# The inverse transform's scratch turned round, and the whole issue order laid out anew

## The chip, the cores and the metric

The kernel runs on one core of a Trainium2 chip. Its time is the device time of one execution in microseconds; 618.68 us is the median of three runs of the kernel before (617.52 to 621.3). One execution was also recorded by the hardware profiler; the views quoted below come from that one.

## The reference, cut to what matters

The result mixes two branches row by row with a gate. One is a long convolution along the sequence (2048 rows, 512 channels) with a kernel K built from a state-space model with 128 states; the other is a gated linear unit with a hidden width of 1792.

```python
g = _sigmoid((x * gate_w).sum(-1, keepdims=True))
# a: the convolution
P = jnp.exp(logdA[:, :, None] * l[None, None, :])
K = jnp.einsum("dn,dnl,dn->dl", Cc, P, dB).real
...
Yf = Uf * Kf[None, :, :, :]
y = irfft2(Yf)[:, :, 0, :L]
a = y + u * Dskip
# b: the gated unit
h = _sigmoid(x @ w_gate) * (x @ w_up)
b = h @ w_down
return g * a + (1 - g) * b
```

## The kernel before, in words

Everything is done in one launch, and the two branches are interleaved instruction by instruction. The gated unit gives TensorE most of its work: `gups` (line 1125) multiplies x by the gate and up weights, `dps` (line 1197) multiplies the hidden tile by the down weights, each as three products of split operands. One turn of `gups` is six matmuls, one turn of `dps` three. Its weights are loaded by SyncE into staging tiles `st` (line 1055) and split into a high and a low part by ScalarE (line 1058) and VectorE (line 1059). The results of four groups of hidden slices are added into `out`: by a plain store, by accumulating DMAs issued from GpSimd (line 1221), and for the second half of the rows in the late groups by VectorE into tiles held in on-chip memory (line 1210; GpSimd and SyncE then don't add there, and SyncE stores the held tile at line 950).

The convolution is a transform of length 2048 made of small matmuls, with three scratch tensors in HBM between its steps:

- `rows` folds and transforms u (PE line 736) and stores the result in `a_u` (line 775).
- `tables` builds the kernel's terms by doubling (VectorE lines 608 to 610, ScalarE line 580) and multiplies them (PE line 652). `second` transforms them (PE line 682) and stores `a_k` (line 694).
- `passes` goes over two halves j of the channels (256 each) and four steps p2. Each step loads its part of `a_u` and `a_k`, finishes both transforms (PE lines 845 and 872), multiplies them (VectorE, from line 885) and does the first step of the inverse (PE line 910). `evict` copies that from PSUM into a tile `ev` (line 354) and stores it in the scratch `b_s` in two transfers of 256 KB (line 930), 32 of them in all.
- `finals` loads `b_s` when all 16 stores of its half j have landed: four blocks `t4`, each as four transfers of 256 KB (line 972), 32 in all. `last` does the last step of the inverse (PE `fps`, line 985), sums and differences on VectorE (lines 996 to 1003), and adds the gated result into `out`, by accumulating DMAs from GpSimd (line 1018) or into the held tiles (line 1008).

`b_s` is indexed by part c, q, j, then k (64 values) and channel. A store takes 64 partitions with four values of k each, which lie side by side: 4 KB without a break per partition. A load takes k on 64 partitions and four values of j, which lie 64 KB apart: four pieces of 1 KB per partition.

The tile `ev` has its own slots, and they are shared: the result tile `mn` of `last` comes out of the same pool of slots (line 991), and so a slot is free for the next `ev` only when the accumulating DMA that reads `mn` has landed.

The order of the instructions is written out by hand in the string `ORDER`: one letter per turn of a strand on an engine. The class `Plan` goes through it; each engine executes its instructions in that order, SyncE and GpSimd issue their DMAs in it. The letters that are spoken of: `d` a turn of `gups`, `e` a turn of `dps`, `#` the inverse step, `+` the `fps` step on TensorE; on SyncE `D` a load of x, `a` a load of the rows u, `E` and `F` a load of the up/gate and down weights, `r` a store into `a_k`, `f` a load of `passes`, `)` a store into `b_s`, `$` a load from `b_s`, `g` a load or store of a held output tile; on GpSimd `2` and `.` accumulating DMAs. `Plan` keeps estimated times beside that; they choose which free slot of a pool is taken, and change nothing else in a given order.

Of the kernel before, what the change touches and what calls it, by code (L numbers as in the profile page):

```python
# [66 lines left out]
ORDER = (
    "DhiABEjEjkddHIEjkDhiddkDhiddEjJkDhiddyEjGZatatazykddattbDhEjEjDkddhbZucZFlkddAEjDykdzdizFihvvcZLdilyLMNzMyDhiddCOFRSOPlQ"
    "OTdzmedmRQEadtmaEQeyzQQayddLxGaxetTOzddQyGtTjyEWEWT0eeeddWjzxOWjWLWzOWtUykdWkWzEPxyQOVW0eeddedVuzWv1EjyQyx0eeWeUkdUWQ1UU"
    "zRdS0eeedTFld0eeeydQWWzWRWkWz1jdv1xTWXT0YjTbEQdyUOseeeddyVVbZ1cxxZEzU1UydUUXkz0vxdRSYxvcdyZaQWdETsjzyWWRedjekdeTxaTdWydd"  # L70
    "zTWWmWzddy0eWkWEUWknoxjVvz1EVWEWzdydWyUdFldyFUUlvpUmezmezdkzyxF1RSqWzyjdxazlmjdedxjTW0ee2eeEjERTyWWWtWXad02tTdkYTdseeeek"
    "dyjzUdMykdNMkzdOVzOPQOtVUUUdU02eLEQeqrQeeEXQkRSdQO0Y2TxtRdjQyWyzdWseWzWOWddeeWOWTyzWeWnWkoPTydQTU02WjdeeedWzVyEEkdVeWzOd"
    "QWWUyzU02UWUQejeee02dWeeFlFdeyldedjFFRSTymWRzWpX02ddybQEYTzTlddTdkdzmUqyzusemyzlmbZVeyzVeUyzUdeqcZj02eQeEvxxUejUeOQRSXk0"
    "2kkTvxRTdYsWWWWdnoWWdxWyzWcWeTyzEWeZaeETUWe02WtWdddataVeVUUeUjee02jWtUWrLadeeRSeed02evxyxWvxzxedTee02pyRTTWWkeWXeetbe02d"
    "TYsqUzMdyzqNMeeFFdeedkVOObPQOVUlUUZUXlF02ddDDmQLQDRScyzQZQdvxYDdTvOmxyRQWzOlWWOddseeWmTdyWWzyeTWnoWWdTUh02PQWzWWcexVVrhd"
    "ee02OQWUvUxdUveUdexWWehpyQxR02SxeWdyeheddxDWqDTRQWWXzyqriiDzT02YTTUQyizzViffffOdVUGDUUUXyzRSQdhiddyhhsYsWThnW45f6WdeRTfW"
    "TiWWiWiWeTWzWdddyd68yd9dUVVe0W2dydzWz%UWUzUWdyWUeedWoyRSue02dyEEj%eeeTRjd02dTT%dLWeeWzWeFlpXdyE02YEf%zqz!TUddseeyVezMNkk"
    "mz01MOdOPeVUeqrQOUUyUjdyXzQde#ffRzSddQE0QQYOjdkTRQWysneeyWWOdddeWzWzdT&WOPW&ETf4Q)T)kWWOWU01Ef1y&Wjde&5yWzeW)dVVkWeEff6d"
    "dyzUUUjkWz68dU0eQ1efe9%yRS0j1)dede%dyEQTRjde%ETdyQTopWWWdWXdz%!0TqzYU1Qqrj#seeyfeVzzkkOkVUUUUdy0zdeeFed&&QfR)SljX0yzTYf)"
    "WmWRWdyz&sFlTWnWk1fWmWdEyzWW4de&dFTdyz5doWTUj66yEff8WWflmdeWzVVWWU1UdUdee02pqyzeeeqe02UW9RSeed%eTRe02de%eTeeW%0yzW%!deWe"  # L80
    "eXedrE)jTk02)#(fYfTU2yzdkj&))fsV4VUded&UeU&UXee0d566yyz2EjdkzEfjYsndop)qdfdqf89%%%yz%kEyddf!dedyekEzedy#ddj)&(Ezr&fff4ff"
    "yffgz(fffe)0)g57689%%%%efF!)dy)dejFddekdyfl4$zf$#(e&z&$ydmd(f5$zz))k*yz6F)l78$fFd+,E0dfye-9-m,,.$%z%%%.dd,,..$E)jk!fdd$j"
    "ddlyzy#z(&mf))f&E4lme*(ydee3+,--,eeeek57,dy7fz3.d.d,fjkj)ffz8k9%%%,..gEjeedef4)fffedydk3g5$6%!eye$68d#(&&(zgefe3))2))$9%"
    "%%%edeedy$!gedd3#&ee2g())zy&()e)g$$$ed3edyz$dzy*+,-z--e*-d$e-d$e3zydy$+,---e$F$-l-d$$--e*Fe$*F+,$$d-eddy+$z-$lzme,me,..l"
    ",meee*,..$ye-$3eez+zee3y,eee-z$ee-,3e3-e3--$g-g--*,+.,ee3eg-e-.e3-e-g--gg3,,..e3gg")
# [243 lines left out]
def body(ctx, tc, xp, xt, prm, ldt, dsk, gw, wgu, wdn, c_wu, c_wf, c_wk, c_wwk, c_wwu, c_wwv, c_pw, out):  # L329
    nc = tc.nc  # L330
    mm, V, A, S = nc.tensor.matmul, nc.vector, nc.scalar, nc.sync
# [587 lines left out]
    def evict(j, p, pi, bd, t):  # L919
        es, = yield fin["ev"], 1  # L920
        ev = es.tile("ev", [P, 4, W])
        te = []
# [4 lines left out]
        end = []
        for r in range(2):
            dst = b_s[j][:, :, :, 8 * p + 4 * r:8 * p + 4 * r + 4].rearrange("c q j k d -> (c q j) k d")
            end.append((yield "SP", kb(280), lambda: S.dma_start(dst, ev[64 * r:64 * r + 64]), [max(te)]))  # L930
# [29 lines left out]
    def finals(j):  # L960
        yield bdone[j]
        yield E["wf"]
        for t4 in range(4):
# [4 lines left out]
            tb = []
            for q in range(2):
                for c in range(2):  # L970
                    src = b_s[j][c, q, 4 * t4:4 * t4 + 4].rearrange("j k d -> k j d")
                    tb.append((yield "SP", kb(360), lambda: S.dma_start(b[64 * c:64 * c + 64, q], src), [sb.t, bdone[j].t]))
# [322 lines left out]
```

## Time and profile before

| What | Value |
|---|---|
| median of three runs | 618.68 us |
| the profiled execution's own time | 619.26 us |
| its span, first to last instruction | 617.5 us |
| TensorE (PE) busy | 587.1 us, 95% |
| VectorE (DVE) busy | 539.2 us, 87% |
| ScalarE (ACT) busy | 411.3 us, 67% |
| moved by DMA | 104.19 MB, 169 GB/s over the span |

A row of a windows view gives, for a stretch of the span, how long each engine was busy, the granted TensorE clock, the mean busy share of the 16 DMA engines (it can pass 1 where packets overlap) and what they moved. The chain of waits starts at the last instruction and goes back, at each step, to what released it. A row that begins with a queue's name (q1 is SyncE's, q0 GpSimd's) gives packets, megabytes and the packets' time as a share of the 16 engines over the window asked for.

### The profile page before, as it was taken

To read this page: it belongs to the slowest core of one execution; us is meant where nothing else is said; L and a number is where in the kernel's file an instruction comes from. 1 tells how busy PE (TensorE), PEld (TensorE's weight loads), DVE (VectorE), ACT (ScalarE), POOL (GpSimd) and SP (SyncE) were. 2 spreads that over 40 slices of the span, in tenths; PEclk is the share of its full clock that TensorE was granted. 3 is DMA by queue.
4 is the path that set the end of the run, shared out by engine and by line. 5 is a ranking of instruction groups with operands and counts; after the bars stand their busy time and mean duration, and the time that the engine had idled before them with its cause. 6 is when DMAs were issued, how large, how long until landed. Compare 5 with 4: busy or idle time off the path is not lost.

```text
span 617.5 us, 16699 instructions
## 1 busy us (share of the span) xinstructions
PE 587.1 (95%) x7147; PEld 449.1 (73%) x7147; DVE 539.2 (87%) x766; ACT 411.3 (67%) x659; POOL 52.9 (9%) x80
## 2 busy tenths in 40 slices
PE   7899999999999998987999999999979997999996
PEld 3688878888887886775787877877757665667774
DVE  4999999999999999999999999999518676856687
ACT  4698878698798679997779988895732242231230
POOL 6000000101101110110010000002000010210021
PEclk9999999999999999999999999999979999999999
DMA  7564434545435783587534872677989998996996
GB/s 234 178 213 136 137 90 151 156 93 138 83 69 122 214 204 75 143 223 165 124 53 132 216 185 93 198 148 159 217 198 217 257 240 190 251 255 175 225 218 171
DMA packets 72236, 104.19 MB, mean 169 GB/s; under 512 B 6113, under 2 KB 44897, under 8 KB 70114
## 3 DMA queue, kind: packets, MB, share of 16 engines
q1 hardware_dynamic: 65250, 92.63, 55.8%
q0 software_dynamic: 6912, 10.49, 12.4%
q8 instruction: 56, 0.92, 0.6%
q14 instruction: 18, 0.15, 0.1%
HBM read 61.15 MB, written 41.95 MB: 167 GB/s over the span
## 4 chain that ended last, share of the span: by engine, by line
PE 73%; DMA 9%; DVE 8%; issue 4%; ACT 4%; SPq 1%; POOL 0%; DVEq 0%; POOLq 0%; ACTq 0%
PE gups L1125 40%; PE dps L1197 19%; PE kps L652 4%; PE wps L682 3%; PE s2k L872 2%; DMA b_s<-ev 2%; DMA st<-wdn 2%; PE s2u L845 2%; PE ips L910 2%; DMA out<-mn 1%; DMA parts<-b_s 1%; PE ups L736 1%; DMA u<-xp 1%; DVE T L610 1%; DVE t L608 1%
## 5 line engine op out<-in xcount | busy, mean ns | idle before, releaser
L1125 PE MATMUL gups<-x,gu 128*128 128x512 f32 x1344 | 334.1, 395 | 6.8 <-DVE gu L1059 2.4
L1125 PEld LDWEIGHTS gups<-x,gu 128*128 128x128 f32 x1344 | 250.0, 189 | 74.1 <-issue 9.9
L1197 PE MATMUL dps<-dnw,h 128*128 128x512 f32 x672 | 174.3, 396 | 4.1 <-DVE dnw L1059 3.5
L1197 PEld LDWEIGHTS dps<-dnw,h 128*128 128x128 f32 x672 | 124.2, 188 | 41.0 <-issue 6.8
L1221 POOL DMA_DIRECT2D out<-part x30 | 26.2, 874 | 401.6 <-ACT part L1216 161.2
L580 ACT ACTIVATE B<-B 128x32 f32<-128x32 f32 (+2 forms) x96 | 53.4, 671 | 0.3
L1174 ACT ACTIVATE h<-sg 128x512 fp32r<-128x512 f32 x56 | 35.1, 627 | 26.2 <-DVE sg L1170 26.2
L1216 ACT ACTIVATE part<-dps,omg 128x512 f32<-128x512 f32 x46 | 31.4, 684 | 25.0 <-PE dps L1197 22.8
L1168 ACT ACTIVATE sg<-gups 128x512 f32<-128x512 f32 x56 | 33.1, 590 | 19.2 <-PE gups L1125 18.0
L610 DVE TENSOR_TENSOR T<-T,t 128x1024 f32<-128x1024 f32 (+3 forms) x48 | 41.7, 870 | 0.1
L608 DVE TENSOR_TENSOR t<-T,bz 128x1024 f32<-128x1024 f32 (+3 forms) x48 | 41.5, 864 | 0.3
L609 DVE TENSOR_TENSOR T<-T,bz 128x1024 f32<-128x1024 f32 (+3 forms) x48 | 41.6, 866 | 0.0
L1175 DVE TENSOR_TENSOR h<-sg,h 128x512 fp32r<-128x512 f32 x56 | 38.3, 686 | 2.3 <-ACT h L1174 2.2
L1058 ACT ACTIVATE gu<-st 128x512 fp32r<-128x512 f32 (+1 forms) x52 | 31.2, 608 | 12.5 <-DMA st<-wgu 11.5
L1170 DVE SCALAR_TENSOR_TENSOR sg<-sg,gups 128x512 f32<-128x512 f32 x56 | 38.1, 682 | 0.0
L652 PEld LDWEIGHTS kps<-B,T 128*32 128x32 f32 x2048 | 29.4, 110 | 10.0 <-issue 5.3
L652 PE MATMUL kps<-B,T 128*32 128x64 f32 x2048 | 31.9, 220 | 4.2 <-DVE B L589 3.8
L1059 DVE TENSOR_TENSOR gu<-st,gu 128x512 fp32r<-128x512 f32 (+1 forms) x52 | 34.1, 666 | 0.0
L354 ACT ACTIVATE ev<-ips 128x512 f32<-128x512 f32 x21 | 12.1, 596 | 29.1 <-PE ips L910 11.4
L498 ACT ACT_TABLE_LOAD x20 | 25.7, 1283 | 0.3
L885 DVE TENSOR_TENSOR tt<-s2k,uf 128x1024 f32<-128x1024 f32 x10 | 12.2, 1225 | 14.9 <-PE s2k L872 14.0
L507 ACT ACTIVATE af<-ex 128x1024 int32<-128x1024 f32 x16 | 16.9, 1056 | 11.5 <-DVE ex L558 11.5
(126 smaller groups left out, 706.7 us busy)
## 6 DMA issues: line engine op xcount, KB each, us to landing
st<-wgu SPq DMA_DIRECT2D x48, 256.0 KB, 4.6
a_u<-evu SPq DMA_DIRECT2D x32, 256.0 KB, 4.5
a_k<-kev SPq DMA_DIRECT2D x8, 1024.0 KB, 6.0
b_s<-ev SPq DMA_DIRECT2D x32, 256.0 KB, 5.3
out<-part POOLq DMA_DIRECT2D x30, 256.0 KB, 4.1
st<-wdn SPq DMA_DIRECT2D x24, 256.0 KB, 4.4
ak<-a_k SPq DMA_DIRECT2D x12, 512.0 KB, 8.6
au<-a_u SPq DMA_DIRECT2D x10, 512.0 KB, 5.7
```

The source lines that it names most:

```text
L580: A.activation(B[:, :, 0, 1 << k::2 << k], B[:, :, 0, 1:64 >> k:2], AF.Exp, scale=float(1 << k))
L608: yield "DVE", c, lambda: V.tensor_tensor(t2, src, sb, op=OP.mult), [t, slot.t]
L609: te = yield "DVE", c, lambda: V.tensor_tensor(dst, src, br, op=OP.mult), [t]
L610: te = yield "DVE", c, lambda: V.tensor_tensor(dst, dst, t2[:, :, ::-1], op=OP.add), [te]
L652: mm(p[32 * jj:32 * jj + 32, s], T[:, 32 * i + ch, c], B[:, ch, c], start=(c == 0), stop=(c == 1), tile_position=(0, 32 * jj), skip_group_ ...
L1059: te = yield "DVE", dve(n), lambda: V.tensor_tensor(lo, st, hi.bitcast(F32), op=OP.subtract), [te]
L1125: mm(p, gu[:, a, k, dc], x[:, b, dc], start=(dc + n == 0), stop=(dc == NC - 1 and n == 2))
L1168: t = yield "ACT", actp(512), lambda: A.activation(sg, pg_, AF.Tanh, scale=0.5), [tg, ss.t]
L1170: t = yield "DVE", dve(512), lambda: V.scalar_tensor_tensor(sg, sg, 1.0, pu, op0=OP.add, op1=OP.mult), [t, tu]
L1174: t = yield "ACT", act(512), lambda: A.activation(h[:, 0], sg, AF.Copy), [t, hs.t]
L1175: t = yield "DVE", dve(512), lambda: V.tensor_tensor(h[:, 1], sg, h[:, 0].bitcast(F32), op=OP.subtract), [t]
L1197: mm(p, h[:, a, 128 * s:128 * s + 128], dn[:, b], start=(f == fs[0] and n == 0), stop=(f == fs[-1] and n == 2))
```

## The change

The scratch `b_s` is declared with k outermost. A store now writes, for each of its 64 partitions, four pieces of 1 KB that lie 64 KB apart (together the store covers 256 KB without a hole); a load reads 4 KB without a break for each of its 64 partitions, which lie 64 KB apart. Number and size of the transfers stay as they were.

In `Plan`, the estimate of a DMA no longer starts as soon as its issuing engine is free: SyncE's and GpSimd's transfers stand in one line, a transfer counts as moving after all that were issued before it, and a transfer may be issued at most 10 us ahead of the last landing of those in line. The sizes by which the estimate counts the two kinds of transfers are altered too (280 to 330 for a store, 360 to 290 for a load). `ORDER` is another string from first to last letter; it holds the same turns (2122 letters), apart from six copies that go from ScalarE to VectorE or back.

```diff
-        self.count, self.used, self.turned, self.moves, self.fetch = 91.0 + 2 * WARM, [0.0] * 1024, False, [], [0.0, 0.0]
+        self.count, self.used, self.turned, self.moves, self.fetch, self.back, self.issued = 91.0 + 2 * WARM, [0.0] * 1024, False, [], [0.0, 0.0], 0.0, 0.0
...
-    b_s = [dr.tile([2, 2, 16, 64, W], F32, name=f"b_s{j}") for j in range(NW)]
+    b_s = [dr.tile([64, 2, 2, 16, W], F32, name=f"b_s{j}") for j in range(NW)]
...
-            dst = b_s[j][:, :, :, 8 * p + 4 * r:8 * p + 4 * r + 4].rearrange("c q j k d -> (c q j) k d")
-            end.append((yield "SP", kb(280), lambda: S.dma_start(dst, ev[64 * r:64 * r + 64]), [max(te)]))
+            dst = b_s[j][8 * p + 4 * r:8 * p + 4 * r + 4].rearrange("k c q j d -> (c q j) k d")
+            end.append((yield "SP", kb(330), lambda: S.dma_start(dst, ev[64 * r:64 * r + 64]), [max(te)]))
...
-                    src = b_s[j][c, q, 4 * t4:4 * t4 + 4].rearrange("j k d -> k j d")
-                    tb.append((yield "SP", kb(360), lambda: S.dma_start(b[64 * c:64 * c + 64, q], src), [sb.t, bdone[j].t]))
+                    src = b_s[j][:, c, q, 4 * t4:4 * t4 + 4]
+                    tb.append((yield "SP", kb(290), lambda: S.dma_start(b[64 * c:64 * c + 64, q], src), [sb.t, bdone[j].t]))
...
-            elif eng == "SP":
+            elif eng in ("SP", "POOL"):
                 m, more = m if isinstance(m, tuple) else (m, 0.0)
-                end = start + 0.44 + more
-                self.free[eng] = end
-                end = max(self.move(end, m / 306e3, start), end + 0.6) + 1.4 + (min(SLACK["dma"], 0.75) if start < 8 else SLACK["dma"])
-            elif eng == "POOL":
-                end = start + 0.95
-                self.free[eng] = end
-                end = max(self.move(end, m / 245e3, start), end + 0.6) + 2.6 + SLACK["dma"]
+                start = max(start, self.back - 10.0 if self.issued else 0.0)
+                end = self.free[eng] = start + (0.44 + more if eng == "SP" else 0.95)
+                self.issued = max(end, self.issued)
+                landed = self.move(self.issued, m / (306e3 if eng == "SP" else 245e3), start)
+                self.back = max(self.back, landed)
+                tail = 1.4 + (min(SLACK["dma"], 0.75) if start < 8 else SLACK["dma"]) if eng == "SP" else 2.6 + SLACK["dma"]
+                end = max(landed, end + 0.6) + tail
```

The first and the last five lines of the string, of 18 each:

```diff
 ORDER = (
-    "DhiABEjEjkddHIEjkDhiddkDhiddEjJkDhiddyEjGZatatazykddattbDhEjEjDkddhbZucZFlkddAEjDykdzdizFihvvcZLdilyLMNzMyDhiddCOFRSOPlQ"
...
-    "eXedrE)jTk02)#(fYfTU2yzdkj&))fsV4VUded&UeU&UXee0d566yyz2EjdkzEfjYsndop)qdfdqf89%%%yz%kEyddf!dedyekEzedy#ddj)&(Ezr&fff4ff"
-    "yffgz(fffe)0)g57689%%%%efF!)dy)dejFddekdyfl4$zf$#(e&z&$ydmd(f5$zz))k*yz6F)l78$fFd+,E0dfye-9-m,,.$%z%%%.dd,,..$E)jk!fdd$j"
-    "ddlyzy#z(&mf))f&E4lme*(ydee3+,--,eeeek57,dy7fz3.d.d,fjkj)ffz8k9%%%,..gEjeedef4)fffedydk3g5$6%!eye$68d#(&&(zgefe3))2))$9%"
-    "%%%edeedy$!gedd3#&ee2g())zy&()e)g$$$ed3edyz$dzy*+,-z--e*-d$e-d$e3zydy$+,---e$F$-l-d$$--e*Fe$*F+,$$d-eddy+$z-$lzme,me,..l"
-    ",meee*,..$ye-$3eez+zee3y,eee-z$ee-,3e3-e3--$g-g--*,+.,ee3eg-e-.e3-e-g--gg3,,..e3gg")
+    "ADhHiEjIKDhDiDhkddEjkddhGZaiBaatiattEtjkddEjkddFblEjmEjkddbZcZDhkFAiyldDhidzEjkCvLLymzvDEFDMcZadyezNMOOdPyzjehQOiktaaddh"
...
+    "&&kdVVUeUdee2zEUfe0yf))jUXdee&&ef4jf5e6E07d2kkzyYsnoz)f)df8pqqdyeEzyfEdj29%%%%ddrfff4fffdyede57z6!d#j&&ed8kzy((09%%%%dye"
+    "EdfEff!)dfeekfzd4f)e)#(0&)dy(dzyj(z5762dfjk89%%%gdje)%$)f!)FelFee$mdyFffddzlm#)l(z&y0&ddzk$f4dfd$yzFy*+ek(d)),Eejme-5lf-"
+    ",,zyf$f$f$6.dy$.,dEj)f)zme789f,3ee%e%%dd*+-dfy4e.kd-Eg56.z%!7d#&3eee&e-,kyd,fg3eeEdf8z)).jk(egyz$e32.&,j,yg$2d)g9d%k%eee"
+    "e3f.).de%eedy%e$!#$*&gz3&((zzgeeed)+de)-$-ddy3ede--e)-z-)-yzyz$$$*yz+F,d$-$$l-$dFd*+,-de-$-l-$F$$-y*$$-$,,$.3*d.lm,mm,zd"
+    "+..,-ede$yz-,,$ee3yezye$3+,eze--e3-ee$-*e.-+-,ee-3-.,,ege3-eg-e.g.g-e3eg-geeee3g3g")
```

More of the change, by code (lines that the diff above doesn't have):

```diff
@@ L67 @@
 ORDER = (
-    "DhiABEjEjkddHIEjkDhiddkDhiddEjJkDhiddyEjGZatatazykddattbDhEjEjDkddhbZucZFlkddAEjDykdzdizFihvvcZLdilyLMNzMyDhiddCOFRSOPlQ"
-    "OTdzmedmRQEadtmaEQeyzQQayddLxGaxetTOzddQyGtTjyEWEWT0eeeddWjzxOWjWLWzOWtUykdWkWzEPxyQOVW0eeddedVuzWv1EjyQyx0eeWeUkdUWQ1UU"
-    "zRdS0eeedTFld0eeeydQWWzWRWkWz1jdv1xTWXT0YjTbEQdyUOseeeddyVVbZ1cxxZEzU1UydUUXkz0vxdRSYxvcdyZaQWdETsjzyWWRedjekdeTxaTdWydd"
-    "zTWWmWzddy0eWkWEUWknoxjVvz1EVWEWzdydWyUdFldyFUUlvpUmezmezdkzyxF1RSqWzyjdxazlmjdedxjTW0ee2eeEjERTyWWWtWXad02tTdkYTdseeeek"
@@ L72 @@
[L72 to L79, printed above, removed]
@@ L80 @@
-    "WmWRWdyz&sFlTWnWk1fWmWdEyzWW4de&dFTdyz5doWTUj66yEff8WWflmdeWzVVWWU1UdUdee02pqyzeeeqe02UW9RSeed%eTRe02de%eTeeW%0yzW%!deWe"
-    "eXedrE)jTk02)#(fYfTU2yzdkj&))fsV4VUded&UeU&UXee0d566yyz2EjdkzEfjYsndop)qdfdqf89%%%yz%kEyddf!dedyekEzedy#ddj)&(Ezr&fff4ff"
-    "yffgz(fffe)0)g57689%%%%efF!)dy)dejFddekdyfl4$zf$#(e&z&$ydmd(f5$zz))k*yz6F)l78$fFd+,E0dfye-9-m,,.$%z%%%.dd,,..$E)jk!fdd$j"
-    "ddlyzy#z(&mf))f&E4lme*(ydee3+,--,eeeek57,dy7fz3.d.d,fjkj)ffz8k9%%%,..gEjeedef4)fffedydk3g5$6%!eye$68d#(&&(zgefe3))2))$9%"
@@ L84 @@
-    "%%%edeedy$!gedd3#&ee2g())zy&()e)g$$$ed3edyz$dzy*+,-z--e*-d$e-d$e3zydy$+,---e$F$-l-d$$--e*Fe$*F+,$$d-eddy+$z-$lzme,me,..l"
-    ",meee*,..$ye-$3eez+zee3y,eee-z$ee-,3e3-e3--$g-g--*,+.,ee3eg-e-.e3-e-g--gg3,,..e3gg")
+    "ADhHiEjIKDhDiDhkddEjkddhGZaiBaatiattEtjkddEjkddFblEjmEjkddbZcZDhkFAiyldDhidzEjkCvLLymzvDEFDMcZadyezNMOOdPyzjehQOiktaaddh"
+    "lidQyQddQQtRSTxmxtOQRduyTWzWEWvdOxEWdzWaxxWLdjkWyzeTOPWWTdUyztxddEW0eyzjkeeE1dddEWWVVUUQOUUWG0eee1jQvxxyzydRWWzd0ejLEeWe"
+    "dG1QSTRyWWzd0edeeWXTbukjQ1yTd0YTkdUEQEFseeeyVzObZVUUUUXkddzRldy1ScZ0Qjvxxv1xdYdWxkWcZTyzWzWydsdeeevdRTydET0jWWzWmWWTnWzE"
@@ new lines @@
+    "axtWUdyyzdoWa1tdzkVddWyzVUUjUyzekFUlamjdeRadeFEEFyzSddvxdWyzddWlmyzT0peReexjlmyTzed02eeWtWWtWXbeTe02dYqTUkMsdyzeEeeeNMdL"
+    "kOd1bOPV0ee2eQOVUUUUXqGQeddQyjkdRSz02QYdQOTRQWsnoeeeydeTjTdjExETErWpy02eeedWOWkWWeOPQWzWWUVVZWOdq0WWkdeWUjQyUeUe2qUzWecR"
+    "SW0deydFQdzeeTRjeWFWWjdQWXzkkTTy02dYElTmUQkOyddzzyjlmdzVVUUFUUXdvvdyyzZcdRsYlZaSQzyTWdskdWWyRFaElExdzWaxzeWddWTnoxyWmTde"
+    "ezdWyWmdjWzyTEWzeWUtvWkWjxrxWk02V2deWeee02jdyeLEEzVUUUkUvyxxeeezRSWa0tpqeee2e0dj2TReeeed0eeT2eWteWkTtX0dbYTUdyqbMjseeedz"
@@ new lines @@
+    "deVdNMkVy0eeFeZOderOPUQyOUzUlUXz2QQ02QRSdQOmdyTRYcZQWFFsenolW2ddDxlDdWmWzedTDyWWTTzyWvxxOvxxWdUWDdzVWcVdmeWdy0e2eWOPQWUO"
+    "UUhevxxddWUhvxxpQh02yWRSQdqTeqWzhRyTWeWrffeWXdfd4Qi0diTiYyTUfQVVDhidzdOzz56U6UdUUXdDdysi2RzSyQhyYsWdzDefeWWiTfudD8hWRedW"
+    "iWnWy0e2zyuWoTW9edzW%WhTWTUddiedy%0ee2dLdeVzd%zypVUUUW0Ufeed2qEEFeW0RS2zWydeeeTRjdqryLdWzWT0eeTWWXez%!d0YT#UfM1dfEfseeed"
+    "yzjyddfNMz4OOPkddkVQOVUUUUXR&SEQQyzQ01YQOTseeeR2QWyddzd&))dWEWjTOWnWTWkWEyTj&OP0ee1Wy&)5fffdd)WUQVVWz6eWWkW0zWUy68deUUdU"
@@ new lines @@
+    "WO1Qoe9eRS%ydQTjWdyd%R%j0edee1ETWWzTQWpXTz%!zQ01YUEkOkqjq#fkfseeelmdyzVfVUUdU&U40eXe&1jkefF)E)RSdyzQ0yzYdWTFRryWWsdnodyW"
+    "zWWlmWTTdzEjWWk&WTUdyWzW&)lddyzWmded5FVddVWUWyU6lmze6yzypqqUfdf8zWWeWde09%UeWRej1Sede0df%TyeR%XE%jT2!eekedr0dYTEs#TzyU2)"
+    "&&kdVVUeUdee2zEUfe0yf))jUXdee&&ef4jf5e6E07d2kkzyYsnoz)f)df8pqqdyeEzyfEdj29%%%%ddrfff4fffdyede57z6!d#j&&ed8kzy((09%%%%dye"
+    "EdfEff!)dfeekfzd4f)e)#(0&)dy(dzyj(z5762dfjk89%%%gdje)%$)f!)FelFee$mdyFffddzlm#)l(z&y0&ddzk$f4dfd$yzFy*+ek(d)),Eejme-5lf-"
```

## The prediction

> **What bounds the kernel now.** I read the page's head first, then the windows, to see where TensorE is not busy:
>
> ```profile
> span 617.5 us, 16699 instructions
> PE 587.1 (95%) x7147; PEld 449.1 (73%) x7147; DVE 539.2 (87%) x766; ACT 411.3 (67%) x659; POOL 52.9 (9%) x80
> ...
> 0.00:20.00 20.00, 14.84 (x49) 8.18 (x49) 11.33 (x23) 11.39 (x22) 10.74 (x32) 1.00 0.75 239
> ...
> 225.00:290.00 65.00, 57.46 (x949) 43.55 (x948) 63.75 (x93) 59.14 (x94) 5.22 (x6) 1.00 0.61 151
> ...
> 450.00:480.00 30.00, 25.33 (x387) 18.84 (x386) 12.53 (x17) 6.99 (x12) 0.00 (x0) 0.89 0.97 205
> 480.00:500.00 20.00, 18.93 (x252) 13.84 (x252) 16.14 (x20) 6.99 (x11) 0.00 (x0) 1.00 1.09 249
> 500.00:524.00 24.00, 19.74 (x220) 13.53 (x219) 15.14 (x21) 8.39 (x17) 3.56 (x4) 0.97 0.93 219
> 524.00:565.00 41.00, 39.55 (x534) 27.57 (x533) 29.82 (x38) 9.26 (x17) 5.28 (x6) 0.97 0.98 234
> 565.00:600.00 35.00, 35.00 (x285) 25.14 (x285) 25.66 (x44) 10.93 (x21) 3.51 (x4) 1.00 1.04 218
> 600.00:617.50 17.50, 11.32 (x77) 8.42 (x75) 13.14 (x24) 2.55 (x6) 3.53 (x4) 0.93 0.68 167
> ```
>
> The columns are the stretch, the busy time of PE, PEld, DVE, ACT and POOL, then the clock, the DMA share and GB/s. TensorE stands still for 617.5 - 587.1 = 30.4 us: 5.2 at the start, 7.5 in 225 to 290, 4.7 + 1.1 + 4.3 + 1.5 = 11.6 between 450 and 565, 6.2 at the end. Its work is not changed, so the change can win these 30.4 us at most. From 450 to 600 the DMA engines are full (0.93 to 1.09). The 11.6 us in that stretch are where transfers decide, and I looked there in the timelines and the chain of waits:
>
> ```profile
> 450.95 4.59 issue
> ...
> 466.35 6.01 SPq L828 DMA_DIRECT2D wwv<-c_wwv  x1
> ...
> 515.98 0.89 POOL L1018 DMA_DIRECT2D out<-mn  x1 [6.99 <-issue]
> ...
> 521.42 1.34 ACT L354 ACTIVATE ev<-ips 128x512 f32<-128x512 f32 x2 [9.02 <-DMA out<-mn]
> ...
> 522.78 2.19 PE L1197 MATMUL dps<-dnw,h 128*128 128x512 f32 x4 [3.49 <-DVE dnw L1059]
> ...
> 567.31 0.45 SPq L930
> ...
> 567.81 4.54 DMA b_s<-ev
> ...
> 588.53 4.67 SPq L972 DMA_DIRECT2D parts<-b_s  x4
> ```
>
> Two incidents. At 450.95 TensorE waits 4.59 us for nothing that the profile shows, in the middle of a step whose operands were there. The row at 466.35 shows SyncE held 6.01 us over one transfer: the line of transfers backs up. At 508.99 GpSimd is held 6.99 us before one accumulating DMA. That DMA reads `mn`, whose slot the next `ev` needs; ScalarE waits 9.02 us for it, everything behind that copy in its queue waits too, the split of a down weight among it, and TensorE stands 3.49 us for that weight.
>
> **The scratch, part by part.** Of 32 stores and 32 loads of 256 KB, the stores go from 64 packets of 4 KB to 256 of 1 KB, the loads the other way. These rows price them; each q1 row belongs to the window 573 to 583, 145 to 160, 80 to 95 and 345.9 to 348.6, in this order, with the transfers issued in it below:
>
> ```profile
> q1 hardware_dynamic: 2168, 2.21, 112.7%
> parts<-b_s SPq DMA_DIRECT2D x8, 256.0 KB, 9.8
> ...
> q1 hardware_dynamic: 432, 0.79, 18.5%
> st<-wdn SPq DMA_DIRECT2D x3, 256.0 KB, 2.8
> ...
> q1 hardware_dynamic: 1586, 2.04, 47.0%
> a_u<-evu SPq DMA_DIRECT2D x4, 256.0 KB, 3.9
> ...
> q1 hardware_dynamic: 110, 0.40, 70.7%
> b_s<-ev SPq DMA_DIRECT2D x2, 256.0 KB, 3.2
> ...
> L930 SPq DMA_DIRECT2D b_s<-ev x32: 445/490/1888, 346.1 to 567.8; - x32
> L972 SPq DMA_DIRECT2D parts<-b_s x20: 573/578/1033, 499.5 to 592.6; - x20
> L775 SPq DMA_DIRECT2D a_u<-evu x32: 574/599/1432, 32.9 to 263.4; - x32
> ```
>
> Loads in 1 KB packets (first window): 2.21 MB in 1.127 x 10 = 11.3 us of all engines, 196 GB/s, or 1.34 us for 256 KB. Loads in 2 KB packets (second): 0.79 MB in 0.185 x 15 = 2.8 us, 0.92 us for 256 KB. No load of 4 KB pieces stands in the trace. One bound is 0.92, as the larger packet should do no worse; the other is the 4 KB stores (fourth): 0.40 MB in 0.707 x 2.7 = 1.9 us, 1.25 us for 256 KB, four packets to each engine as the new loads have. I take 0.92, the row of the same direction: 0.42 us less per load, 13.4 us of engine time for 32, of which 6.7 falls to the 16 loads of the second half. By the other end it is 0.09 each, 1.4 us for these 16.
>
> The Trainium skill, "DMA: Bandwidth & Descriptors", Specifications, gives 512 B as the smallest transfer for line rate; by that, 1 KB and 4 KB packets move alike and the layout is worth nothing. The trace disagrees here, 196 GB/s against 285 for 2 KB pieces.
>
> Stores in 1 KB packets exist: `a_u<-evu` (third window). Of its 2.04 MB about 1.07 are 2 KB packets, at the second window's rate 3.8 us; that leaves 3.3 us for 0.97 MB, 0.89 us for 256 KB, against 1.25 for the 4 KB stores of the fourth. So between 0.36 us won per store and, if the fourth window shows latency rather than occupation and a full line would move them as the 2 KB loads at most, about nothing. I take nothing. On SyncE a store costs 599 instead of 490 ns to issue and a load the reverse, 578 to 490: 32 x (0.109 - 0.088) = 0.7 us more of SyncE's time, hidden in its idle time; without that cover it delays the transfer behind each by 0.1 us.
>
> **The order.** The string itself shows the sequence of turns, not their times; what it moves is read from that.
>
> First incident. In the window 450 to 456 the line was full, and one packet of instructions went through beside it:
>
> ```profile
> q1 hardware_dynamic: 1555, 1.36, 113.6%
> q8 instruction: 1, 0.02, 1.5%
> ```
>
> I suppose, and cannot show, that TensorE waited for its instructions behind those transfers. The longest run of SyncE's turns without a turn of TensorE between falls from 14 (`)&(Ezr&fff4ff` and on into the next line) to nine (`$$F$$$$$$`, late in the list), so full stretches should be shorter; where the next packet of instructions falls in them the string doesn't tell. I count half, 2.3 us.
>
> Second incident. It is the fourth of the first four `.` turns. Those stand together before (`.$%z%%%.dd,,..$E`) and come apart in the new list (`.dy$.`, and two alone further on), with loads between. I count the stretch's 4.3 us as gone.
>
> The 1.1 and 1.5 us left between 480 and 565 are short waits in the same full stretch, out of which the loads take up to 13.4 us of engine time: half gone, 1.3.
>
> Against it: the first weight load stands fourth instead of third on SyncE, and two x loads of 256 KB come before the second one, where `E` followed at once. At the start's 239 GB/s two such loads take 2.2 us; half of it lies beside the split work that TensorE waits for there anyway, so 1.0 us lost. The 7.5 us of 225 to 290 and the 6.2 at the end I leave: TensorE's turns behind the last `fps` grow from 7 to 12, but the adds that follow the last matmul remain.
>
> The sum: 2.3 + 4.3 + 1.3 - 1.0 = 6.9 us off the span, 610.6. The profiled execution took 619.26, 1.8 outside its span, and lies 0.6 above the median, so 1.2 is added: 611.8, rounded **612**.
>
> **What decides whether it is kept: the tail.** The last store into `b_s` is followed by 10 turns `d`, 33 `e` and six `fps` before, by 7, 25 and five after.
>
> ```profile
> 557.24 1.36 PE dps L1197 x6
> 558.60 1.36 PE gups L1125 x6
> ...
> 605.25 1.09 PE L985 MATMUL fps<-parts,wf 64*32 64x256 f32 x32
> ```
>
> With 1.36 us for a `d`, 0.68 for an `e` and about 1.09 for `fps`, that is 42.6 us of TensorE's work before and 32.0 after. The store moves 10.6 us later against TensorE. The chain behind it took 617.5 - 567.8 = 49.7 us, 20.8 of them between its landing (572.4) and the last load's issue (593.2). In the forecast the store is issued at 567.8 + 10.6 - 6.9 = 571.5, so the chain may take 610.6 - 571.5 = 39.1. It has 6.7 us less of loads and some 4 us less for the landing of the last one (9.8 in the first window above, against an estimated 6): 49.7 - 10.7 = 39.0. It just fits, and that makes the forecast fragile.
>
> **The rivals.**
>
> The loads are no faster in 4 KB pieces, or only by the low end. Then the chain takes 49.7 - 1.4 = 48.3 and ends at 571.5 + 48.3 = 619.8, time **621**: the tail gives back what the middle won. For it: the 4 KB stores at 1.25 us, with the same four packets per engine. Against it: the old stores had the spacing of the new loads, 64 KB from partition to partition, and while four of them were under way the rate was up to 389 GB/s:
>
> ```profile
> GB/s 0 0 0 0 0 0 0 0 143 205 266 123 246 164 164 226 287 389 266 123 41 205 348 348 369 328 307 185 215 164 205 113 236 287 364 364 369 364 215 174
> ```
>
> (the window 565 to 573 in 40 slices.) The Trainium skill, same page, "Latency and other measured facts", lists copies between HBM tensors whose rows lie a power of two apart: 207 GB/s at 512 KiB, 103 at 4 MiB. Its list doesn't go down to 64 KB, and the trace shows no such loss there.
>
> Slower: none of the two standstills goes, since neither was a matter of the listed bursts, and the tail binds. The last store is then issued at 567.8 + 10.6 = 578.4, the chain of 48.3 us ends at 626.7, time **628**. It decides as soon as the chain behind the last store takes over 617.5 - 578.4 = 39.1 us without anything won ahead of it. For it: before, TensorE was 100% busy from 565 to 600, so the old list had kept work over for that chain, and the new one keeps 10.6 us less.
>
> Better: with less in the line, the 7.5 us of 225 to 290 shrink too and the tail is fed early; 4 us of those and the other halves, 2.3 + 1.3, give 611.8 - 7.6, or **604**. Nothing in the profile speaks for it but the room.
>
> **How the numbers follow.** Forecast, 607 to 614: 0.38. Better, below 607: 0.13. Loads no faster, or new standstills in place of the old ones, 614 to 624: 0.31. Slower, above 624: 0.18. A measurement of this kernel tells about 1% from no change, 612.5 to 624.9. Faster by more than that are the better case and most of the forecast, 0.13 + 0.30 = 0.43; slower are the slower case without its edge, 0.17; within 1% the rest, 0.40. The range leaves out the last part of the better case and the last of the slower one: 603 to 627; the forecast's own is 607 to 614.
>
> **What would show it.** Two rows of the page answer to the layout alone:
>
> ```profile
> b_s<-ev SPq DMA_DIRECT2D x32, 256.0 KB, 5.3
> ...
> b_in<-b_s SPq DMA_DIRECT2D x12, 256.0 KB, 8.5
> ```
>
> Right: the windows from 450 to 565 of the changed kernel show about 4 us of TensorE standing still instead of 11.6; no matmul step there is broken by 4 us; no copy into `ev` waits for an `out<-mn`; the loads' row comes to 5 to 7 us, at 285 GB/s or so while only such loads move; from the last store's issue to the end about 39 us. Wrong: new rows in which TensorE waits for `fps` operands or for instructions after 570, a landing of the new loads near 9 us, or stores whose landing rises from 5.3 us so far that `ev` slots run out. Standstills of TensorE in the first 300 us that before did not have would be the new list's own, which I did not price beyond the start.

## The result, and the profile after

The changed kernel takes 615.26 us in the median against 618.91 of the kernel before measured beside it (18 runs of each). One of the changed kernel's 18 runs took 2361.38 us; it is left out of the ratio, and without it the median is 615.10. The ratio is 0.9938, with a 95% interval of 0.9916 to 0.996: 0.6% faster, 3.8 us. The forecast was 612, its range 603 to 627. The profiled execution has a span of 613.7 us.

The head of the page and the windows view of the changed kernel (columns as in the prediction):

```profile
span 613.7 us, 16714 instructions
PE 592.2 (96%) x7147; PEld 450.6 (73%) x7147; DVE 541.2 (88%) x768; ACT 408.1 (67%) x657; POOL 52.8 (9%) x80
...
0.00:20.00 20.00, 16.92 (x45) 9.26 (x46) 12.92 (x24) 8.83 (x15) 10.70 (x32) 1.00 0.74 226
...
225.00:290.00 65.00, 63.86 (x864) 50.04 (x864) 62.56 (x94) 58.06 (x96) 4.35 (x5) 1.00 0.70 168
...
400.00:450.00 50.00, 47.80 (x827) 35.84 (x830) 39.81 (x45) 31.64 (x50) 4.34 (x5) 1.00 0.76 173
450.00:480.00 30.00, 28.09 (x435) 20.07 (x423) 17.64 (x20) 8.39 (x13) 0.86 (x1) 1.00 1.00 233
...
500.00:524.00 24.00, 24.00 (x302) 17.28 (x301) 17.88 (x26) 8.65 (x16) 2.64 (x3) 1.00 1.09 232
524.00:565.00 41.00, 38.82 (x414) 28.23 (x413) 26.82 (x36) 9.80 (x19) 6.16 (x7) 0.96 0.90 206
```

Between 450 and 565 TensorE stands still 1.9 + 2.2 = 4.1 us (480 to 500 is full as well), where it was 11.6 and about 4 were forecast. The 7.5 us of 225 to 290 are down to 1.1. Against that, TensorE now waits 1.5 us between 20 and 225 and 6.6 between 290 and 450, where before it hardly ever did.

Standing still isn't the whole account: TensorE is 5.0 us longer busy for the same 7147 matmuls. Busy time is modelled and holds slow matmuls too. So I counted work instead: the matmuls of each line done by a given time, times what one takes at full speed in the chain of waits (for six of `gups` 1.36 us, for three of `dps` 0.68, and so on for the other lines). This table is worked out from those counts:

| by us of the span | before | changed | lead of the changed kernel |
|---|---|---|---|
| 100 | 87.5 | 84.8 | -2.7 |
| 225 | 210.4 | 205.7 | -4.7 |
| 290 | 264.3 | 267.7 | +3.4 |
| 450 | 420.3 | 414.1 | -6.2 |
| 480 | 441.9 | 440.0 | -1.9 |
| 524 | 478.0 | 481.8 | +3.8 |
| 565 | 514.8 | 517.1 | +2.3 |
| 600 | 548.0 | 550.6 | +2.6 |

The new string is behind by 6.2 us of work at 450. Then it wins 10 us in 74, and the rest of its 3.8 us comes out of a shorter end.

Each column is one execution. The same count in the traces of three kernels of the next section shows how far that carries. The two others with the old string (the layout alone, the estimates alone) have done 417.7 and 415.8 us of work at 450 and 508.6 and 509.6 at 565; the other one with the new string (the string alone) has done 412.3 and 514.6. So the loss up to 450 lies between 1.7 and 8 us, and the gain from 450 to 565 between 8 and 12.

What is left of the two incidents, in the timeline of TensorE and the waits:

```profile
452.33 1.09 PE L682 MATMUL wps<-wk,kst 32*64 32x128 f32 x52 [1.59 <-issue]
540.67 0.40 PE L1197 MATMUL dps<-dnw,h 128*128 128x512 f32 x1 [2.04 <-issue]
...
ACT ev L354 <- DMA b_s<-ev: 6.9, 2, 5.9
```

The first incident is there, 1.59 us instead of 4.59 (in other traces of this string it is longer, as the experiments show). The second isn't: no copy into `ev` waits for an `out<-mn` any more. ScalarE waits at that copy for the stores into `b_s` now, 6.9 us in all, and TensorE doesn't feel it.

### The profile page after: what moved, and what is told of

It reads as the page before. It is cut to its first block, busy times and chain, and to the rows that moved or that the text cites. A ratio compares the mean times of both kernels' runs of the same rounds, so it can differ in the third digit from the quotient of the medians.

```text
span 613.7 us, 16714 instructions
## 1 busy us (share of the span) xinstructions
PE 592.2 (96%) x7147; PEld 450.6 (73%) x7147; DVE 541.2 (88%) x768; ACT 408.1 (67%) x657; POOL 52.8 (9%) x80
## 4 chain that ended last, share of the span: by engine, by line
PE 51%; DVE 19%; DMA 11%; ACT 11%; issue 5%; POOL 2%; SPq 1%; DVEq 0%; ACTq 0%; POOLq 0%
PE gups L1125 26%; PE dps L1197 14%; PE kps L652 4%; DMA parts<-a_u 3%; DMA au<-a_u 3%; DVE t L608 2%; DVE T L609 2%; PE wps L682 2%; DVE T L610 2%; PE s2k L872 2%; PE s2u L845 2%; PE ips L910 1%; DMA b_in<-b_s 1%; ACT L537 1%; ACT L498 1%
## 5 line engine op out<-in xcount | busy, mean ns | idle before, releaser
L1221 POOL DMA_DIRECT2D out<-part x32 | 28.3, 884 | 437.7 <-ACT part L1216 406.6
L1216 ACT ACTIVATE part<-dps,omg 128x512 f32<-128x512 f32 x48 | 32.7, 681 | 33.5 <-PE dps L1197 33.5
L1058 ACT ACTIVATE gu<-st 128x512 fp32r<-128x512 f32 (+1 forms) x48 | 29.0, 607 | 5.3 <-DMA st<-wgu 5.3
L1059 DVE TENSOR_TENSOR gu<-st,gu 128x512 fp32r<-128x512 f32 (+1 forms) x48 | 31.3, 661 | 0.3 <-ACT gu L1058 0.3
L585 DVE TENSOR_TENSOR B<-B,ex 128x1024 f32<-128x1024 f32 x16 | 19.5, 1219 | 6.7 <-ACT B L580 6.7
L574 DVE TENSOR_TENSOR B<-pp,pw 128x1024 f32<-128x1024 f32 x16 | 19.6, 1228 | 4.1 <-PE kps L652 4.1
```

The source lines that it names most:

```text
L1216: te = yield "ACT", act(512) + 0.1, lambda: A.activation(part, p, AF.Copy, scale=omg[:, t:t + 1]), [tp, gate[t, 1].t, ss.t]
```

## The experiments

Each ratio is to the kernel before, measured beside the kernel in question on the same chip.

**Layout and string apart.** The layout alone: in the kernel before, three lines.

```diff
-    b_s = [dr.tile([2, 2, 16, 64, W], F32, name=f"b_s{j}") for j in range(NW)]
+    b_s = [dr.tile([64, 2, 2, 16, W], F32, name=f"b_s{j}") for j in range(NW)]
...
-            dst = b_s[j][:, :, :, 8 * p + 4 * r:8 * p + 4 * r + 4].rearrange("c q j k d -> (c q j) k d")
+            dst = b_s[j][8 * p + 4 * r:8 * p + 4 * r + 4].rearrange("k c q j d -> (c q j) k d")
...
-                    src = b_s[j][c, q, 4 * t4:4 * t4 + 4].rearrange("j k d -> k j d")
+                    src = b_s[j][:, c, q, 4 * t4:4 * t4 + 4]
```

> The kernel before with the scratch turned round and nothing else: old string, old estimates. My theory: the gain of 0.6% is the new string's, and the layout only shortens the loads (1.34 us of engine time for 256 KB before, about 1.1 in the changed kernel). Before, TensorE was 100% busy from 565 to 600 beside these loads, so this alone gives little: 617 to 619 us, ratio 0.997 to 1.000. Rival A, the layout is the whole gain: 615 us, ratio 0.994. Rival B, the 1 KB stores cost more than the loads win: 620 to 622 us, ratio above 1.002. In the profile: a store issue row of about 600 ns instead of 490, a load issue row of about 490 instead of 580, loads landing about 2 us sooner.

Measured: 621.74 us, ratio 1.0028 (0.9998 to 1.0059). No gain; rival A is out. The median lies where rival B put it, but between "nothing" and "a little slower" the interval doesn't decide.

The string alone: the same three lines taken back in the changed kernel.

> The changed kernel with the old scratch: new string, new estimates, loads again in 1 KB pieces. My theory by the prediction's tail step: the last 16 loads take 16 x 0.24 = 3.9 us longer, and as the chain behind the last store just fits, most of that is seen: 618 to 619 us against 615.3, so almost no gain over the kernel before. Rival A, the string is the whole gain and the loads are hidden: 615 to 616 us, ratio 0.994 to 0.996. Rival B, the string alone is a loss that the layout repays: over 620 us.

Measured: 616.8 us, ratio 0.9958 (0.9937 to 0.998). My own theory fell: the last loads were 4 us of engine time longer, and the median rose by 1.5 us, which the two intervals don't tell from nothing. The string makes the gain, all of it or most of it.

The prices of the two kinds of transfers can now be read. First the rows of the changed kernel's window 579 to 588, then the same stage with the old layout (583 to 592 of the string alone), in which SyncE's queue moves hardly anything but these loads and some 2 KB packets:

```profile
q1 hardware_dynamic: 789, 2.26, 105.0%
parts<-b_s SPq DMA_DIRECT2D x8, 256.0 KB, 8.1
```

```profile
q1 hardware_dynamic: 1893, 1.96, 111.8%
parts<-b_s SPq DMA_DIRECT2D x8, 256.0 KB, 9.3
```

2.26 MB in 1.05 x 9 = 9.45 us are 239 GB/s, 1.10 us for 256 KB; 1.96 MB in 10.06 us are 195 GB/s, 1.34 us. A load in 4 KB pieces saves 0.25 us of engine time. The traces with the old string agree: 195 GB/s for the 1 KB packets before, 241 for the 4 KB packets of the layout alone, in the 14 us around the last loads. For the stores, the first two of the layout alone (window 347.6 to 350.3; the prediction has the 4 KB stores at the same place, 0.40 MB at 70.7%):

```profile
q1 hardware_dynamic: 255, 0.44, 78.7%
b_s<-ev SPq DMA_DIRECT2D x2, 256.0 KB, 3.3
...
L930 SPq DMA_DIRECT2D b_s<-ev x32: 574/615/1447, 347.8 to 574.4; - x32
```

The row gives 207 GB/s against 209, but it isn't stores alone: by the sizes in the trace, 27 of the 255 packets are 8 KB packets of another transfer (17 of the 110 before), half of the bytes here and a third before. The last four stores, counted by packet size, are cleaner: 256 packets of 4 KB took 240 ns each in the kernel before (565 to 573), 1024 packets of 1 KB took 62 ns each with the layout alone (571 to 581). That is 0.96 and 1.00 us of engine time per store. In 1 KB pieces a store costs the DMA engines about what it cost before, and 615 ns of SyncE instead of 490.

**The estimates alone.** The changed kernel with the old string: layout and new `Plan`, which can then only pick other slots.

```diff
 ORDER = (
-    "ADhHiEjIKDhDiDhkddEjkddhGZaiBaatiattEtjkddEjkddFblEjmEjkddbZcZDhkFAiyldDhidzEjkCvLLymzvDEFDMcZadyezNMOOdPyzjehQOiktaaddh"
+    "DhiABEjEjkddHIEjkDhiddkDhiddEjJkDhiddyEjGZatatazykddattbDhEjEjDkddhbZucZFlkddAEjDykdzdizFihvvcZLdilyLMNzMyDhiddCOFRSOPlQ"
...
```

> The changed kernel with the old string: layout and new estimates stay, so the estimates can only choose other free slots. My theory: slots matter where a tile waits for a slow transfer (the copy into ev that waited 9.0 us for an accumulating DMA), and in the old string those four DMAs still stand together, so the incident stays and the time is that of the layout alone, 617 to 619 us. Rival: the choice of slots, not the string, took the incident away: 615 to 616 us, and no copy into ev waits for out<-mn.

Measured: 619.75 us, ratio 1.0008 (0.9983 to 1.0032); the copy into `ev` waits 10.1 us for an `out<-mn`, and the wait for `dnw` is there with 3.45 us. The choice of slots does nothing that can be measured.

**The second incident.** The eight accumulating DMAs that read `mn` left out, in either kernel:

```diff
             for i in range(2):
                 t = 4 * t4 + k[i]
+                if slot is es:
+                    done.append(max(t1))
+                    continue
                 done.append((yield "POOL", kb(215), lambda: nc.gpsimd.dma_start(out[t, :, cols], y[:, i], accum_op=OP.add), [max(t1), begun[t]]))
```

> The kernel before without the eight accumulating DMAs that read mn (1 MB of 104): half of the first half's rows don't get their convolution part. It takes away the wait of the copy into ev for such a DMA. If the second incident of the prediction is what it was taken for, TensorE's 3.5 us wait for dnw near 522 is gone, with its slower clock behind it: 4 to 5 us, 614 to 615 us against 619. Rival: the copy is late for another reason, or the tail takes it back: 618 to 619 us.

> The changed kernel without the same eight DMAs. If the new string has already removed that wait, little is left: 614 to 615.5 us against 615.3, and most of it from 1 MB less in the line. Rival: as much is won as in the kernel before, 610 to 611 us, so the new string didn't remove it.

Measured: 614.81 us from the kernel before, ratio 0.9943 (0.9912 to 0.9974), and 615.18 from the changed one, 0.9955 (0.9922 to 0.9987), where that one itself has 0.9938. What is worth 4 us in the old string is worth nothing that can be measured in the new one, though 1 MB less moves in both. The window around it, of the kernel before and then of the kernel before without these DMAs:

```profile
480.00:524.00 44.00, 38.67 (x471) 27.37 (x471) 31.28 (x41) 15.38 (x27) 3.56 (x4) 0.99 1.00 233
```

```profile
480.00:524.00 44.00, 42.15 (x561) 29.78 (x567) 33.11 (x44) 16.71 (x29) 1.78 (x2) 1.00 1.07 254
```

Without the eight DMAs TensorE stands still 1.9 us there instead of 5.3.

**The first incident.** The loads of `a_k` (512 KB each) from consecutive addresses, in either kernel:

```diff
-                    tk.append((yield "SP", (kb(720), 0.2), lambda: S.dma_start(dst, src[r]), [sk.t, kdone[j].t]))
+                    tk.append((yield "SP", (kb(720), 0.2), lambda: S.dma_start(dst, a_k[j][p2, 64 * r:64 * r + 64].rearrange("p (o x) d -> p o (x d)", x=8)), [sk.t, kdone[j].t]))
```

> The kernel before with the loads of a_k (16 x 512 KB) taken from consecutive addresses, 8 KB per partition instead of pieces of 512 B: the same bytes, but the regrouping is left out, so the convolution is wrong. The line near 450 is full of these short pieces. If TensorE's 4.59 us wait for nothing that is shown is a wait for instructions behind that line, it shrinks to under 2 us and the granted clock of the window 450 to 480 comes back from 0.89: 612 to 615 us. Rival: the wait has nothing to do with the line and stays near 4.6 us: 616 to 619 us, by the shorter loads alone.

> The changed kernel with the loads of a_k from consecutive addresses in the same way. Its own waits of this kind are 1.59, 2.04 and 1.68 us: if they are fetches behind the line, most of the 5 us go, 609 to 612 us. Rival: 614 to 615 us.

Measured: 618.37 us, ratio 0.997 (0.994 to 0.9999), and 613.96 us, 0.9927 (0.9896 to 0.9959). The waits in the same step `wps`, of the kernel before and of the changed one with these loads:

```profile
458.38 1.83 PE L682 MATMUL wps<-wk,kst 32*64 32x128 f32 x80 [2.69 <-issue]
```

```profile
454.42 1.97 PE L682 MATMUL wps<-wk,kst 32*64 32x128 f32 x52 [3.45 <-issue]
```

In the one the wait is 2.69 us instead of 4.59, in the other 3.45 instead of 1.59. Before this is put down to the loads, the same wait in the other traces has to be seen (one of the kernels comes further down). The last column is how long the granted clock stands at 0.50 from about the end of the wait on.

| string | kernel | wait in `wps`, us | clock at 0.50, us |
|---|---|---|---|
| old | before | 4.59 | 6.8 |
| old | layout alone | 4.89 | 6.8 |
| old | estimates alone | 4.43 | 6.8 |
| old | without the `mn` DMAs | 4.34 | 6.8 |
| old | consecutive `a_k` | 2.69 | 3.4 |
| new | changed | 1.59 | 0 |
| new | string alone | 3.79 | 6.8 |
| new | half of the loads | 2.01 | 3.4 |
| new | without the `mn` DMAs | 0.86 | 0 |
| new | consecutive `a_k` | 3.45 | 6.8 |

With the old string the consecutive loads give the one short wait of five, which speaks for my theory that the length of the line sets it. With the new string the wait is anything from 0.86 to 3.79 us when these loads are as they were, so 3.45 says nothing against the theory. One trace of each doesn't settle it, and the time of the kernel before, 618.37, stayed in the rival's range. The table also shows that the wait's 1.59 us in the changed kernel is a low value of a wide spread.

What TensorE probably waits for can be seen. In the kernel before and in the changed one, windows of 1 us (452 to 453 and 449 to 450):

```profile
q8 instruction: 1, 0.02, 9.3%
```

```profile
q8 instruction: 1, 0.02, 6.0%
```

One packet of instructions moves shortly before the wait ends. In the traces of the first ten kernels TensorE has 24 waits of more than 0.9 us "for issue"; in each, one packet of that queue begins 2.2 to 3.0 us before the wait's end, and no other in the 4 us before that. Most of these waits come again at the same steps in the traces of one string, with other lengths: near 413, 454 and 541 us with the new string, near 458 and 552 with the old. That fits a fixed place in TensorE's list of instructions at which the next block is late; that TensorE waited for this packet is inferred from the times. The Trainium skill, "Runtime: NRT & Kernel Launch", Instruction fetch mechanics, says that instructions come in blocks of 16 KiB through a DMA queue of their own, and that the cost of crossing a block is mostly hidden. The profile's page counts 56 packets with 0.92 MB, 16 KB each, and by this reading the cost wasn't hidden 24 times in ten traces. What delays the packet, the line or the moment at which it is asked for, stays open.

**How far the tail is bound by loads.** Half of the loads from `b_s` left out in the changed kernel:

```diff
-            for q in range(2):
+            for q in range(1):
                 for c in range(2):
                     src = b_s[j][:, c, q, 4 * t4:4 * t4 + 4]
...
-                        mm(ph[32 * jj:32 * jj + 32, c, q ^ c], wf[rr, q], b[rr, q, jj], start=True, stop=True,
+                        mm(ph[32 * jj:32 * jj + 32, c, q ^ c], wf[rr, q], b[rr, 0, jj], start=True, stop=True,
```

> The changed kernel with half of the loads of the inverse's scratch left out: the part q = 1 isn't loaded, and the last step multiplies the part q = 0 twice. 16 transfers of 256 KB fewer, 8 of them behind the last store. If the loads bind the tail (the prediction's step: the chain behind the last store just fits), it ends 8 x 1.1 = 9 us of engine time sooner, of which I expect 3 to 6 us before TensorE's own work binds: 609 to 612 us. If TensorE's remaining work binds already: 614 to 615.5 us.

Measured: 612.71 us, ratio 0.9893 (0.9862 to 0.9924), between the two forecasts. 16 loads fewer win 2.6 us by the medians. In the traces the span is 3.5 us shorter; 1.9 us of that is work already done by 565, so the 9 us of engine time behind the last store are worth some 1.6. TensorE waits for nothing behind 565 in either trace. The tail is bound by TensorE's remaining work first; loads reach through it only in part. The chain of waits of the changed kernel does run through a hold of GpSimd before an `mn` DMA at 588.36, but without these DMAs, and so without the hold, the time was the same (615.18).

**Which half of the string.** Strings put together: one kernel's first letters, then the other's string without the turns already taken (each letter is "the next one of its kind", so a joined string does the same work, apart from a few copies that change engine). First the old head, up to where TensorE stands near 225 and near 450 us, on the new tail, then the new head on the old tail. Only `ORDER` differs from the changed kernel:

```diff
 ORDER = (
-    "ADhHiEjIKDhDiDhkddEjkddhGZaiBaatiattEtjkddEjkddFblEjmEjkddbZcZDhkFAiyldDhidzEjkCvLLymzvDEFDMcZadyezNMOOdPyzjehQOiktaaddh"
+    "DhiABEjEjkddHIEjkDhiddkDhiddEjJkDhiddyEjGZatatazykddattbDhEjEjDkddhbZucZFlkddAEjDykdzdizFihvvcZLdilyLMNzMyDhiddCOFRSOPlQ"
...
```

> The changed kernel with the old string's first 822 letters (to where TensorE stands near 225 us), then the new string without the turns already taken. In the two traces TensorE has done 4.7 us less work at 225 in the changed kernel than in the one before, 6.2 us less at 450, and 2.6 us more at 600. Theory: the loss of the head is real and can be had back: 611 to 614 us, ratio 0.988 to 0.992. Rival: VectorE, 98% busy until 400 in both, sets the pace there and the head's lead melts before 450: 615 to 617 us, ratio 0.993 to 0.997. A joint that fits badly could make it slower than both.

> The changed kernel with the old string to where TensorE stands near 450 us (1609 letters), then the new one. Theory, the gain of the change lies between 450 and 565 alone and everything before is a loss of 6 us: 609 to 613 us. Rival, the work that the new head has done earlier by then (tables, transforms) is what makes the middle run: 617 to 621 us, the old standstills come back behind the joint.

> The other half: the new string to where TensorE stands near 450 us (1597 letters), then the old one. Theory of the middle: the old incidents (the copy into ev behind an accumulating DMA, 3.5 us) come back on top of the head's loss: 621 to 625 us. Rival, the head makes the gain: 614 to 616 us.

Measured: 629.36 us, ratio 1.0169 (1.0139 to 1.0199), for the old head up to 225; 619.29 us, 1.0006 (0.9986 to 1.0025), up to 450; 621.52 us, 1.004 (1.0017 to 1.0062), for the new head on the old tail. None beats the changed kernel. The work done, by the same count:

| by us | before | changed | old head to 450 | new head, old tail |
|---|---|---|---|---|
| 450 | 420.3 | 414.1 | 417.5 | 412.4 |
| 480 | 441.9 | 440.0 | 432.6 | 440.5 |
| 524 | 478.0 | 481.8 | 474.9 | 477.3 |
| 565 | 514.8 | 517.1 | 512.7 | 512.5 |
| 600 | 548.0 | 550.6 | 546.4 | 546.2 |

```profile
457.26 2.39 PE L682 MATMUL wps<-wk,kst 32*64 32x128 f32 x68 [5.66 <-issue]
```

```profile
525.65 1.77 PE L1197 MATMUL dps<-dnw,h 128*128 128x512 f32 x4 [1.61 <-DVE dnw L1059]
```

With the old head (first row) the first incident is back, 5.66 us, and by 480 the kernel is 7.4 us behind the changed one. With the old tail (second row) the copy into `ev` waits 9.1 us for an `out<-mn` again and TensorE for `dnw`; from 0.5 us ahead of the changed kernel at 480 it falls to 4.6 behind at 565. So the second part of the gain lies in the tail of the string. That the first part lies in the head rests on one trace, of a wait that varies. The loss of the new head couldn't be had back this way: with the old head up to 225, TensorE waits 5.42 us for an `a_u` load behind the joint, at 286 us, and whether the loss can be had back at all stays open.

**GpSimd's descriptors.**

```diff
-        ("st", 5, [P, 512], F32),
+        ("st", 4, [P, 512], F32),
...
-    nc = bacc.Bacc("TRN2", target_bir_lowering=False, num_devices=1, dynamic_dma_scratch_size=1024)
+    nc = bacc.Bacc("TRN2", target_bir_lowering=False, num_devices=1, dynamic_dma_scratch_size=2048)
```

> The changed kernel with 2048 instead of 1024 bytes for the descriptors of GpSimd's DMAs, paid for with one staging tile of five. In both traces GpSimd issues three accumulating DMAs in a row and is held 6 to 7 us before the fourth (508.99 before, 588.36 in the changed kernel, where the chain of waits runs through it). If it is held for room for descriptors, the fourth follows at once and the tail is 2 to 4 us shorter: 611 to 613 us, less what the missing staging tile costs. Rival, it is held by what the DMA itself waits for: 615 to 617 us and the hold stays.

Measured: 719.58 us, ratio 1.1646 (1.1596 to 1.1697), so as a version it is useless; I suppose that the missing staging tile costs this, but nothing here tells the two edits apart. The hold can be read all the same. GpSimd's timeline, of the changed kernel and then of this one:

```profile
585.69 1.77 POOL L1018 DMA_DIRECT2D out<-yt  x2 [35.27 <-ACT yt L1014]
587.01 1.35 POOL L1018 DMA_DIRECT2D out<-mn  x1
594.47 0.86 POOL L1018 DMA_DIRECT2D out<-mn  x1 [6.11 <-ACT h L1174]
```

```profile
688.48 1.75 POOL L1018 DMA_DIRECT2D out<-yt  x2 [36.26 <-ACT yt L1014]
689.93 2.09 POOL L1018 DMA_DIRECT2D out<-mn  x2
```

With 1024 bytes the fourth in a row is held 6.11 us (the releaser that the row names writes another tile, which this DMA doesn't read); with 2048 it follows at once. In the kernel before, the fourth in a row is held three times: 6.99 us, the second incident, then 5.65 and 3.92. That fits a hold for room. It isn't shown, since the run with 2048 bytes was another one in time and in its line of transfers too.

## Why the prediction was right or wrong

**The direction and the range held; the point was 3 us too low.** 6.9 us were forecast off the span, 3.8 came. The likeliest case by its own bounds (607 to 614) was missed by 1.3 us, and the time fell within 1% of before. It fell into the band of the rival "loads no faster, or new standstills in place of the old ones" (614 to 624, chance 0.31): the loads were faster, but new standstills did come. The range reached from some 16 us below the kernel before to 8 above it, so that it held says little.

**The middle was right.** Forecast: 2.3 for the first incident, 4.3 for the second, 1.3 for short waits, 7.9 in all between 450 and 565. By the work done it was 8.5 us (from -6.2 to +2.3), and 8 to 12 by the other traces. The second incident was what it was taken for: leaving out the DMAs that read `mn` is worth 4 us before and nothing after, and in all traces with the old second half of the string a copy into `ev` waits 9 to 10 us for such a DMA (unless these are left out), in none with the new one. The first incident came out at 1.59 of 4.59, which was luck: where the loads of `a_k` are as they were, the new string has 0.86 to 3.79 us there, 2.1 in the mean of four traces, and the old one 4.34 to 4.89. Half of it gone, as forecast, is a fair reading of that, but the reason given for it, shorter full stretches of the line, isn't shown. What the incident cost was undersized, since I counted the standstill alone. The chain of waits of the kernel before shows what follows it:

```profile
455.54 2.44 PE wps L682 x80
457.98 4.52 PE gups L1125 x12
```

Twelve `gups` otherwise take 2.72 us; 4.52 is 1.8 more, and 80 of the 128 `wps` of 2.02 us should take 1.26 and took 2.44. That is 3.0 us on top of 4.59, in a stretch (454.5 to 461.3) whose granted clock is 0.50. After the changed kernel's 1.59 us the clock stays at 1.00.

**The start and what I left unpriced were wrong, and this is the step that failed in the sum.** I took 1.0 us off for the start and left 225 to 290 alone. The new string was 2.7 us of work behind at 100, 4.7 at 225 and 6.2 at 450. Part of the 2.7 is not the string's order but the clock at the start. These are rows of TensorE's first matmuls, of the kernel before and of the changed one:

```profile
9.22 4.18 PE L1125 MATMUL gups<-x,gu 128*128 128x512 f32 x17 [0.23 <-DVE x L1059]
```

```profile
8.98 4.40 PE L1125 MATMUL gups<-x,gu 128*128 128x512 f32 x10 [0.58 <-DVE gu L1059]
```

A matmul takes 0.25 us in the one and 0.44 in the other. The windows view gives 1.00 for the clock of both, but the changed kernel's trace has no record of the clock before 13 us. In the two other traces of the old string, which have such a slow stretch at 9 to 14 us, 86.8 and 85.9 us of work are done at 100 instead of 87.5; the new string has 84.8 and 83.9. So the order costs some 2 us there, twice what I took.

The new string did win most of the 7.5 us (from -4.7 to +3.4 at 290), and lost them again, to -2.5 at 400 and -6.2 at 450. TensorE waits 6.6 us between 290 and 450: 3.3 for ScalarE, 0.6 for VectorE, 0.7 for loads and 1.9 for nothing that the profile shows, 1.68 of them at once at 413. VectorE is busy 98% of 20 to 400 in both strings (373.0 and 373.5 of 380 us by the windows); I read the standstill of 225 to 290 as TensorE's, to be had by transfers, in a stage that VectorE paces. That this is the reason is argued from the busy shares and not shown by a run, and it can hold only up to 400: from 400 to 450 VectorE is busy 80%, and the last 3.7 us are lost there.

**The layout's size was off, within its bounds.** Taken: 0.42 us saved per load, bounds 0.09 and 0.42; measured 0.25. The end of the sum that was taken came from another stage: the 2 KB loads at 0.92 us moved while the queue took 18.5% of the engines, and in the full window of 573 to 583 the 2 KB packets cost as much per byte as the 1 KB ones beside them (199 and 198 GB/s). So 196 against 285 GB/s compared a full line with a nearly empty one. The other end, 1.25 us, came from a window with another transfer's packets in it. Stores: nothing taken, 0.04 us measured in engine time. By the rule of 512 B in the Trainium skill, "DMA: Bandwidth & Descriptors", Specifications, the layout would be worth nothing. In time nothing could be measured (1.0028, 0.9998 to 1.0059); in engine time the traces of this case disagree, 195 against 239 GB/s in a full line.

**The tail was read wrongly.** I let the last store move 10.6 us later against TensorE, because 10 `d` and 33 `e` follow it in the old string and 7 and 25 in the new. The two lines' matmuls after the last store's issue, of the kernel before and of the changed one, first `gups`, then `dps`:

```profile
567.80:617.50 49.70, 14.82 (x60) 10.81 (x58) 0.97 0.95 208
567.80:617.50 49.70, 24.35 (x96) 17.47 (x96) 0.97 0.95 208
```

```profile
567.00:613.70 46.70, 16.50 (x66) 12.16 (x66) 1.00 0.86 211
567.00:613.70 46.70, 21.40 (x87) 16.10 (x87) 1.00 0.86 211
```

Before, 60 / 6 = 10 and 96 / 3 = 32 turns, where the string has 10 and 33; after, 11 and 29 where it has 7 and 25. With 1.36 and 0.68 us a turn that is 35.4 against 34.7 us, so the store came 0.7 us later, not the 9.5 that these two kinds of turns make in the string. A letter's place orders an engine's own queue; SyncE issues when the operands are there, and it was some 9 us ahead of TensorE compared with the string. The chain behind the last store took 46.7 us, not 39.1, and that was no harm. So the rival "loads no faster, 621" and the slower one, 628, which both hung on this step, were priced too high: with the new string on the old layout the loads were no faster, and it took 616.8.

**What would have shown it** worked in part: the standstill of 450 to 565 (4.1, about 4 forecast) and the `ev` copies came as written. Three signs didn't: the loads landed in 8.3 us (`b_in`) and 6.7 (`parts`) by the trace instead of 5 to 7, moved at 239 GB/s instead of 285, and the tail took 46.7 us instead of 39. The standstills in the first 300 us that were named as the new list's own came in part, 1.5 us up to 225, and mostly later.
